# First layer of an attention and two-layer MoE kernel: the high and low part of g taken one step later, pieces of x every three steps

## The chip, the cores and the metric

The kernel runs on one core of a Trainium2 chip. The metric is the device time of one execution in microseconds; the time of the kernel before is the median of three runs. TensorE, VectorE, ScalarE and GpSimd are called PE, DVE, ACT and POOL in the rows of the profile, SyncE (which issues most DMAs) SP.

## The reference

Three pieces follow each other. Attention with a feature map: q and k (8 batches, 8 heads, 576 positions, 64 wide) go through exp(+p - max) and exp(-p + max) of p = x @ w_phi, and the output is num / den. The result is x, 4608 tokens by 512. The **first layer**, in which the change lies, is

```
h = x @ w_in           # 4608 x 2048
g = h - tanh(h)
y = g @ w_out          # 4608 x 512
```

The second layer computes ((y @ w1) * (y @ w2)) @ w3 @ w_out2. All of it is fp32.

## The kernel before, in words

A product in fp32 is made of three matmuls with operands of a rounded type (float32r): each operand is split into a high part (a copy into the rounded type) and a low part (the rest), and high x high, low x high, high x low are added up in PSUM.

The first layer (`moe1`) works through 9 blocks of 512 tokens, and in each through 16 chunks of 128 columns of h; one chunk of one block is a step, n = 0 to 143. In step n, TensorE gets `mm1(n)` (L456: 12 matmuls, x and w_in give the tile h(n), 128x512, in one of three PSUM banks) and then `mm2(n - 2)` (L522: 12 matmuls that add g(n-2) @ w_out to four y banks; the four gl matmuls come last, except in the first and last chunk of a block). At the end of a block the four y banks are copied out, three by ScalarE and one by VectorE (`y_out`, L508; three buffers `yo`), and stored to DRAM. The last two steps hold two tiles of the next product, `w34` (L682), in the place of mm1.

Between them lies `act_g` (L479), which makes g: ScalarE takes u = h*h (L485), t = tanh(h) (L486), s (L487) and the mask m (L488); VectorE takes t = h - t (L491), then u by two operations (L492, L494; a polynomial for small h) and puts u into t where the mask says so (L495). Then ScalarE copies t into its high part gh (L503), and GpSimd subtracts gh from t to get the low part gl (L504). u and t have two buffers, s and m one, gh two, gl three.

The order of each engine's work is the order in which the program is written; nothing reorders it. Beside g, each step carries "extras" from a table by step (`extra`): the conversion and splitting of the weights of both layers, in pieces of 128x256. Of these, ScalarE's operations (L105, L120, L127, and L566 for the high part of a split) are issued in `act_g` before gh; VectorE's (L109, L112, L115), GpSimd's (L123 adds, L570 low parts, L589 to L598 sums) and SyncE's (loads of raw weights, stores of w at L601 and L620) are issued after `act_g`. In steps 14 to 77 groups of seven steps combine weights for the second layer (`combos`): on GpSimd four adds, four sums and seven splits for each group. Later steps split single pieces.

Last in a step comes the next block's x, in four pieces. Piece k is loaded in chunk 4k (`load_x`, one DMA for the numerators and two or four for the reciprocals of the denominators, from SyncE's queue into single buffers xn and xr), multiplied on GpSimd in chunk 4k + 1 (L875) and split in chunk 4k + 2 (`split_x`: high part on ScalarE, L881; low part on GpSimd, L882). The last split is thus issued in chunk 14. The first tile of the next block needs all four pieces.

Of the kernel before, what the change touches and what calls it, by code (L numbers as in the profile page):

```python
# [9 lines left out]
F32R = mybir.dt.float32r  # L10
# [42 lines left out]
def kernel(ctx, tc, qk_in, v_in, w_phi, w_in, w_out, w12, w3t_in, wo2, out):  # L53
# [24 lines left out]
    def space(kind, i, shape, dt=F32R):  # L78
        if kind == "x":
            pool = xpools[i // NK]  # L80
        else:
            pool = wpool if i < FC_EARLY else late[0]
        return pool.tile(shape, dt, tag=f"{kind}{i}", name=f"{kind}{i}")
# [51 lines left out]
    def fc_view(t):  # L135
        return t.rearrange("p k f -> p (k f)")
# [319 lines left out]
    def mm1(n):  # L456
        j, i = divmod(n, NFC)
        hh[n] = mm_x(xs[j], slots["in", i], "h")
# [11 lines left out]
    def moe1():  # L470
        with ExitStack() as es:
            p1 = es.enter_context(tc.tile_pool(name="m1", bufs=1))
            p2 = es.enter_context(tc.tile_pool(name="m2", bufs=2))
            p3 = es.enter_context(tc.tile_pool(name="m3", bufs=2))
            ps_y = es.enter_context(tc.tile_pool(name="ps_y", bufs=1, space=PSUM))

            gg, yy = {}, {}

            def act_g(n, ys):  # L479
                h = hh[n]  # L480
                u = p2.tile([128, 512], F32, tag="u", name="u")
                s = p1.tile([128, 512], F32, tag="s", name="s")
                t = p2.tile([128, 512], F32, tag="t", name="t")
                m = p1.tile([128, 512], F32, tag="m", name="m")
                ACT.activation(u, h, ACTF.Square)  # L485
                ACT.activation(t, h, ACTF.Tanh)  # L486
                ACT.activation(s, u, ACTF.Square, bias=c1_sb)  # L487
                ACT.activation(m, u, ACTF.Relu, bias=lim_sb, scale=-1.0)  # L488
                for d in range(3):
                    y_out(ys, d)  # L490
                DVE.tensor_tensor(t, h, t, ALU.subtract)  # L491
                DVE.scalar_tensor_tensor(u, h, C2, u, ALU.mult, ALU.mult)  # L492
                y_out(ys, 3)
                DVE.scalar_tensor_tensor(u, s, C0, u, ALU.add, ALU.mult)  # L494
                DVE.copy_predicated(t, m.bitcast(U32), u)  # L495

                x = extra.get(n, [])
                for f in x:
                    if f in on_act:
                        f()  # L500
                gh = p3.tile([128, 512], F32R, tag="gh", name="gh")
                gl = p3.tile([128, 512], F32R, tag="gl", name="gl", bufs=3)
                ACT.activation(gh, t, ACTF.Copy)  # L503
                POOL.tensor_tensor(gl, t, gh.bitcast(F32), ALU.subtract)  # L504
                del hh[n]
                gg[n] = gh, gl

            def y_out(ys, d):  # L508
                if ys is None:
                    return  # L510
                j, pss = ys
                if d == 3 and j == NB - 1:
                    t = p2.tile([128, 512], F32, tag="t", name="t")
                else:
                    t = p1.tile([128, 512], F32, tag="yo", name="yo", bufs=3)
                if d < 3:
                    ACT.activation(t, pss[d], ACTF.Copy)
                else:
                    DVE.tensor_copy(t, pss[d])
                (ACT if d < 3 else SP).dma_start(y_d[d * 128:(d + 1) * 128, j * 512:(j + 1) * 512], t)  # L520

            def mm2(n):  # L522
                j, i = divmod(n, NFC)
                if i == 0:
                    yy[j] = [ps_y.tile([128, 512], F32, tag=f"y{d}", name=f"y{d}") for d in range(NK)]
                wh, wl = slots["out", i]
                gh, gl = gg.pop(n)
                todo = [(d, m) for d in range(NK) for m in range(3)]
                if 0 < i < NFC - 1:

                    todo.sort(key=lambda a: a[1] == 2)
                for d, m in todo:
                    w, x = ((wh, gh), (wl, gh), (wh, gl))[m]
                    PE.matmul(  # L534
                        yy[j][d], w[:, d * 128:(d + 1) * 128], x,
                        start=i == 0 and m == 0, stop=i == NFC - 1 and m == 2,
                    )
                return (j, yy.pop(j)) if i == NFC - 1 else None
# [3 lines left out]
            cw = 256  # L542
# [17 lines left out]
            def split(of, store):  # L560
                o2 = {}

                def s_hi():
                    t = of()
                    w = o2["w"] = p2.tile([128, 2, cw], F32R, tag="w", name="w")
                    ACT.activation(w[:, 0], t, ACTF.Copy)  # L566

                def s_lo():
                    w = o2["w"]
                    POOL.tensor_tensor(w[:, 1], of(), w[:, 0].bitcast(F32), ALU.subtract)  # L570

                def s_store():
                    store(o2["w"].bitcast(F32))

                on_act.add(s_hi)
                return [[s_hi, s_lo, s_store]]
# [71 lines left out]
            n_all = NB * NFC  # L648
            LAG = 2
            for n in range(n_all + LAG):  # L650
                j, i = divmod(n, NFC)
                if n < n_all:
                    mm1(n)
                else:
                    w34(n - n_all)
                ys = mm2(n - LAG) if n >= LAG else None
                if n >= n_all:
                    for d in range(4):
                        y_out(ys, d)
                if n < n_all:  # L660
                    act_g(n, ys)
                    for f in extra.get(n, []):
                        if f not in on_act:
                            f()
                    if j + 1 < NB:
                        if i % 4 == 0:
                            xa = load_x(j + 1, i // 4)
                        if i % 4 == 1:
                            mul_x(*xa)
                        if i % 4 == 2:  # L670
                            split_x(j + 1, i // 4, xa[0])
                    if j + 1 == NB and i == 2:
                        load_b(0)
                i = n - (n_all - NFC + 1)
                if 0 <= i < NFC:
                    w3t[i] = space("wi", i, [128, 8, 128])
                    SP.dma_start(fc_view(w3t[i]).bitcast(F32), w3t_d[i % 2][i // 2])
                i -= LAG
                if 0 <= i < 8:
                    slots["wo2", i] = slot("wo", i, [128, DM])  # L680
                    for e in range(2):
                        SP.dma_start(slots["wo2", i][e].bitcast(F32), wo2_d[e][i])  # L682

    def w34(i):
        ps = ps_h.tile([128, 512], F32, tag="h", name="h")
        th, tl = w3t.pop(2 * i), w3t.pop(2 * i + 1)
        m = 0
        for j in range(8):
            xh, xl = slots["wo2", j]
            for a, x in ((th, xh), (tl, xh), (th, xl)):  # L690
                PE.matmul(ps, a[:, j, :], x, start=m == 0, stop=m == 23)
                m += 1
        hl = slots["w34", i] = slot("wo", 8 + i, [128, DM])
        ACT.activation(hl[0], ps, ACTF.Copy)
        DVE.tensor_tensor(hl[1], ps, hl[0].bitcast(F32), ALU.subtract)
# [149 lines left out]
    with tc.manual_schedule():  # L845
# [5 lines left out]
        hh, ab_ps, w3t, pending = {}, {}, {}, []  # L851
# [5 lines left out]
        def load_x(j, kk):  # L857
            a = xn.tile([128, 512], F32, tag="xn", name="xn")
            r = xn.tile([128, 512], F32, tag="xr", name="xr")
            c0 = j * 512  # L860
            SP.dma_start(a, num_d[kk * 128:(kk + 1) * 128, c0:c0 + 512])
            done = 0
            while done < 512:
                bp, o = divmod(c0 + done, PT)
                n = min(512 - done, PT - o)
                for e in range(2):
                    SP.dma_start(
                        r[e * D:(e + 1) * D, done:done + n],
                        rden_d[bp, 2 * kk + e:2 * kk + e + 1, o:o + n].to_broadcast([D, n]),
                    )  # L870
                done += n
            return a, r

        def mul_x(a, r):
            POOL.tensor_tensor(a, a, r, ALU.mult)  # L875

        def split_x(j, kk, a):
            hi, lo = slot("x", NK * (j % 2) + kk, [128, 512])
            for e, p in enumerate(xs.setdefault(j, [[None] * NK, [None] * NK])):
                p[kk] = (hi, lo)[e]  # L880
            ACT.activation(hi, a, ACTF.Copy)  # L881
            POOL.tensor_tensor(lo, a, hi.bitcast(F32), ALU.subtract)  # L882
# [56 lines left out]
```

## Time and profile before

| what | value |
|---|---|
| median of 3 runs | 1845.81 us (1845.61 to 1847.29) |
| the profiled execution's own time | 1846.37 us |
| its span | 1844.3 us |
| TensorE busy | 1761.6 us, 96% of the span |
| VectorE, ScalarE, GpSimd busy | 1078.6, 881.5, 902.2 us |

The span runs from the first to the last instruction of the profiled execution; its own time has some 2 us around that. Busy times are sums over stages with different limits. For a change in one stage the waits of that stage have to be read. The granted clock of TensorE is a share of its upper level, 2.4 GHz.

### The profile page before, as it was taken

The page shows a single profiled execution, that of the slowest core. Times are in us where ns is not written, and L with a number is a line of the kernel's source. Part 1 is how long each engine was busy: PE and PEld are TensorE (multiplying, and loading weights), DVE is VectorE, ACT ScalarE, POOL GpSimd, SP SyncE. Part 2 cuts the span into 40 slices and gives each one's busy share as a digit, 9 for nine tenths or more (in the row PEclk, how much of TensorE's full clock was granted, in tenths as well). Part 3 has the DMA queues.
Part 4 walks back from the last instruction along what each step waited for, and adds up shares of the span by engine and source line. Part 5 has one row for each costly group of instructions (what it writes and reads, how often), then busy time and mean ns, then how long its engine had stood idle before and what let it go on. Part 6 is the DMA issues. An engine that isn't in the chain of part 4 may idle for free.

```text
span 1844.3 us, 29297 instructions
## 1 busy us (share of the span) xinstructions
PE 1761.6 (96%) x10464; PEld 1447.3 (78%) x10464; DVE 1078.6 (58%) x1728; ACT 881.5 (48%) x1775; POOL 902.2 (49%) x902
## 2 busy tenths in 40 slices
PE   7999899999998989899999999999999999999999
PEld 5666666668777777677878777888999999999998
DVE  6777787747666656656666766552444444444442
ACT  4656566647656565656666766552121212121211
POOL 5767677726465655655554545231333333333321
PEclk9999999999999999999999999999999999999999
DMA  4444445422223232233334342634647474747461
GB/s 154 144 146 152 148 154 175 125 56 70 70 97 109 97 107 94 96 105 100 121 107 122 103 120 92 228 112 144 204 151 238 151 238 150 236 151 239 151 204 64
DMA packets 143200, 254.68 MB, mean 138 GB/s; under 512 B 18384, under 2 KB 48464, under 8 KB 143056
## 3 DMA queue, kind: packets, MB, share of 16 engines
q1 hardware_dynamic: 139008, 245.68, 41.8%
q10 hardware_dynamic: 4048, 7.15, 1.1%
q8 instruction: 83, 1.36, 0.3%
q14 instruction: 61, 0.50, 0.1%
HBM read 196.89 MB, written 55.87 MB: 137 GB/s over the span
## 4 chain that ended last, share of the span: by engine, by line
PE 50%; issue 14%; POOL 11%; DVE 10%; ACT 8%; DMA 6%; SPq 2%; POOLq 0%; DVEq 0%; ACTq 0%
PE o L796 11%; PE pb L748 8%; PE pa L748 5%; PE pc L748 5%; PE y L534 4%; PE p L200 3%; PE h L465 3%; PE o L331 3%; POOL gl L504 3%; POOL w L570 2%; DVE u L494 2%; DVE t L495 2%; POOL et L123 2%; PE kv L278 2%; PE o L340 2%
## 5 line engine op out<-in xcount | busy, mean ns | idle before, releaser
L465 PE MATMUL h<-x,wi 128*128 128x512 f32 x1728 | 420.9, 391 | 28.1 <-POOL x L882 20.2
L465 PEld LDWEIGHTS h<-x,wi 128*128 128x128 f32 x1728 | 324.4, 188 | 102.1 <-POOL x L882 23.7
L504 POOL TENSOR_TENSOR gl<-t,gh 128x512 fp32r<-128x512 f32 x144 | 186.4, 1294 | 411.2 <-ACT gh L503 385.1
L534 PE MATMUL y<-gh,wo 128*128 128x512 f32 x1152 | 308.3, 403 | 15.6 <-ACT gh L503 13.0
L534 PEld LDWEIGHTS y<-gh,wo 128*128 128x128 f32 x1152 | 219.7, 193 | 75.2 <-ACT gh L503 26.1
L787 POOL TENSOR_TENSOR c<-c,c 128x384 f32<-128x384 f32 x48 | 67.6, 1408 | 322.6 <-DVE c L785 322.6
L491 DVE TENSOR_TENSOR t<-h,t 128x512 f32<-128x512 f32 x144 | 99.6, 692 | 203.8 <-ACT t L486 203.8
L503 ACT ACTIVATE gh<-t 128x512 fp32r<-128x512 f32 x144 | 90.9, 631 | 231.0 <-DVE t L495 228.1
L748 PE MATMUL pb<-wi,w 128*128 128x384 f32 x864 | 173.8, 335 | 3.3 <-DVE u L775 3.3
L534 PE MATMUL y<-gl,wo 128*128 128x512 f32 x576 | 165.4, 394 | 0.7 <-POOL gl L504 0.7
L748 PEld LDWEIGHTS pb<-wi,w 128*128 128x128 f32 x864 | 151.8, 188 | 5.6 <-DVE u L775 5.6
L207 DVE TENSOR_REDUCE m<-p 128x4 f32<-128x512 f32 (+1 forms) x145 | 98.7, 681 | 78.1 <-PE p L200 77.9
L492 DVE SCALAR_TENSOR_TENSOR u<-h,u 128x512 f32<-128x512 f32 x144 | 99.6, 692 | 70.6 <-ACT m L488 70.6
L220 ACT ACTIVATE kp<-dk 128x512 f32<-128x512 f32 x144 | 83.0, 626 | 109.1 <-DVE dk L209 77.7
L494 DVE SCALAR_TENSOR_TENSOR u<-s,u 128x512 f32<-128x512 f32 x144 | 128.2, 890 | 4.6
L534 PEld LDWEIGHTS y<-gl,wo 128*128 128x128 f32 x576 | 110.5, 192 | 24.9 <-POOL gl L504 1.1
L495 DVE COPY_PREDICATED t<-m,u 128x512 f32<-128x512 uint32 x144 | 125.8, 874 | 4.9
L748 PE MATMUL pa<-wi,w 128*128 128x384 f32 x576 | 116.4, 336 | 0.0
L748 PE MATMUL pc<-wi,w 128*128 128x384 f32 x576 | 115.3, 334 | 0.0
L775 DVE TENSOR_TENSOR u<-pb,c 128x384 f32<-128x384 f32 x48 | 26.8, 558 | 147.9 <-PE pb L748 138.1
L302 POOL TENSOR_TENSOR ks<-ks,kp 128x256 f32<-128x256 f32 x128 | 96.4, 779 | 21.3 <-ACT kp L220 21.3
L262 ACT ACTIVATE qp<-tr 128x512 f32<-128x512 f32 (+2 forms) x224 | 84.2, 446 | 45.3 <-PE tr L241 24.7
(104 smaller groups left out, 3130.0 us busy)
## 6 DMA issues: line engine op xcount, KB each, us to landing
w<-w_d SPq DMA_DIRECT2D x336, 256.0 KB
qk<-in_qk SPq DMA_DIRECT2D x33, 576.0 KB
w_d<-w SPq DMA_DIRECT2D x56, 256.0 KB
v<-in_v SPq DMA_DIRECT2D x32, 320.0 KB
num_d<-st SPq DMA_DIRECT2D x128, 72.0 KB
xn<-num_d SPq DMA_DIRECT2D x36, 256.0 KB
x<-y_d SPq DMA_DIRECT2D x24, 384.0 KB
out<-o SPq DMA_DIRECT2D x36, 256.0 KB
```

Source lines behind the costliest of these rows:

```text
L207: DVE.tensor_reduce(m[:, :n], what[g][:, j], AX.X, ALU.max, apply_absolute_value=True)
L302: POOL.tensor_tensor(s, kp[m // G][:, :, m % G, :] if t < 4 else s, x, ALU.add)
L465: PE.matmul(ps, a[:, kk, :], b[kk], start=m == 0, stop=m == 3 * NK - 1)
L491: DVE.tensor_tensor(t, h, t, ALU.subtract)
L492: DVE.scalar_tensor_tensor(u, h, C2, u, ALU.mult, ALU.mult)
L494: DVE.scalar_tensor_tensor(u, s, C0, u, ALU.add, ALU.mult)
L495: DVE.copy_predicated(t, m.bitcast(U32), u)
L503: ACT.activation(gh, t, ACTF.Copy)
L504: POOL.tensor_tensor(gl, t, gh.bitcast(F32), ALU.subtract)
L534: PE.matmul(yy[j][d], w[:, d * 128:(d + 1) * 128], x, start=i == 0 and m == 0, stop=i == NFC - 1 and m == 2,)
L748: PE.matmul(ps, w[:, a, c], x[b][:, kk, :], start=start and m == 0, stop=m == 5, skip_group_check=True)
L796: PE.matmul(ps, a[:, cols], w, start=i == 0 and m == 0, stop=i == 7 and m == 2)
```

## The change

In `act_g` the copy gh and the subtraction gl are cut out and put into a function of their own, `g_parts(n)`. `act_g(n)` calls `g_parts(n - 1)` right after its own four ScalarE operations, ahead of the y copies and of the extras. After the last step `g_parts` is called once more, behind the first tile of the next product and ahead of `mm2`. gl has two buffers now, w three. The pieces of x are loaded, multiplied and split in chunks 3k, 3k + 1 and 3k + 2, so that the last split is issued in chunk 11.

```diff
@@ -474,7 +474,7 @@
             p3 = es.enter_context(tc.tile_pool(name="m3", bufs=2))
             ps_y = es.enter_context(tc.tile_pool(name="ps_y", bufs=1, space=PSUM))
 
-            gg, yy = {}, {}
+            gg, yy, tt = {}, {}, {}
 
             def act_g(n, ys):
                 h = hh[n]
@@ -486,6 +486,7 @@
                 ACT.activation(t, h, ACTF.Tanh)
                 ACT.activation(s, u, ACTF.Square, bias=c1_sb)
                 ACT.activation(m, u, ACTF.Relu, bias=lim_sb, scale=-1.0)
+                g_parts(n - 1)
                 for d in range(3):
                     y_out(ys, d)
                 DVE.tensor_tensor(t, h, t, ALU.subtract)
@@ -498,11 +499,17 @@
                 for f in x:
                     if f in on_act:
                         f()
+                del hh[n]
+                tt[n] = t
+
+            def g_parts(n):
+                if n < 0:
+                    return
+                t = tt.pop(n)
                 gh = p3.tile([128, 512], F32R, tag="gh", name="gh")
-                gl = p3.tile([128, 512], F32R, tag="gl", name="gl", bufs=3)
+                gl = p3.tile([128, 512], F32R, tag="gl", name="gl")
                 ACT.activation(gh, t, ACTF.Copy)
                 POOL.tensor_tensor(gl, t, gh.bitcast(F32), ALU.subtract)
-                del hh[n]
                 gg[n] = gh, gl
 
             def y_out(ys, d):
@@ -562,7 +569,7 @@
 
                 def s_hi():
                     t = of()
-                    w = o2["w"] = p2.tile([128, 2, cw], F32R, tag="w", name="w")
+                    w = o2["w"] = p2.tile([128, 2, cw], F32R, tag="w", name="w", bufs=3)
                     ACT.activation(w[:, 0], t, ACTF.Copy)
 
                 def s_lo():
@@ -653,6 +660,8 @@
                     mm1(n)
                 else:
                     w34(n - n_all)
+                if n == n_all:
+                    g_parts(n - 1)
                 ys = mm2(n - LAG) if n >= LAG else None
                 if n >= n_all:
                     for d in range(4):
@@ -663,12 +672,12 @@
                         if f not in on_act:
                             f()
                     if j + 1 < NB:
-                        if i % 4 == 0:
-                            xa = load_x(j + 1, i // 4)
-                        if i % 4 == 1:
+                        if i % 3 == 0 and i < 12:
+                            xa = load_x(j + 1, i // 3)
+                        if i % 3 == 1 and i < 12:
                             mul_x(*xa)
-                        if i % 4 == 2:
-                            split_x(j + 1, i // 4, xa[0])
+                        if i % 3 == 2 and i < 12:
+                            split_x(j + 1, i // 3, xa[0])
                     if j + 1 == NB and i == 2:
                         load_b(0)
                 i = n - (n_all - NFC + 1)
```

## Rows read from the trace of the kernel before

**Rows 1.** Windows: length, busy time of PE, PEld, DVE, ACT, POOL, clock, DMA share, GB/s
```profile
387.37:1254.17 866.80, 822.43 (x3509) 662.87 (x3505) 541.17 (x865) 540.27 (x1080) 453.41 (x452) 0.98 0.33 106
472.40:1147.22 674.82, 636.02 (x2689) 509.94 (x2688) 434.18 (x696) 430.60 (x872) 377.21 (x384) 0.97 0.32 103
```

**Rows 2.** Timeline of PE at the layer's start: start us, us, what
```profile
401.54 2.88 PE L465 MATMUL h<-x,wi 128*128 128x512 f32 x12
404.26 1.98 PE L534 MATMUL y<-gh,wo 128*128 128x512 f32 x8
406.98 2.88 PE L465 MATMUL h<-x,wi 128*128 128x512 f32 x12
```

**Rows 3.** Waits of PE in the layer: us in total, times, longest us
```profile
PE h L465 <- POOL x L882: 20.2, 8, 4.5
PE y L534 <- ACT gh L503: 13.0, 16, 1.9
PE h L465 <- ACT x L881: 7.9, 8, 1.6
PE y L534 <- DVE yo L519: 2.4, 3, 1.4
```

**Rows 4.** Timeline of PE: the first and the eighth block border
```profile
472.40 2.20 PE L465 MATMUL h<-x,wi 128*128 128x512 f32 x9
478.67 3.19 PE L534 MATMUL y<-gh,wo 128*128 128x512 f32 x8
483.02 2.92 PE L465 MATMUL h<-x,wi 128*128 128x512 f32 x12
...
1147.22 2.20 PE L465 MATMUL h<-x,wi 128*128 128x512 f32 x9
1156.22 2.88 PE L465 MATMUL h<-x,wi 128*128 128x512 f32 x12
```

**Rows 5.** Waits of ACT in the layer
```profile
ACT gh L503 <- DVE t L495: 228.1, 130, 3.9
ACT w L566 <- DMA w_d<-w: 58.9, 38, 2.9
```

**Rows 6.** Timeline of ACT: one step
```profile
749.05 0.63 ACT L503 ACTIVATE gh<-t 128x512 fp32r<-128x512 f32 x1 [1.70 <-DVE t L495]
...
750.06 0.59 ACT L486 ACTIVATE t<-h 128x512 f32<-128x512 f32 x1
...
751.15 0.72 ACT L488 ACTIVATE m<-u,cs 128x512 f32<-128x512 f32 x1
...
754.22 0.63 ACT L503 ACTIVATE gh<-t 128x512 fp32r<-128x512 f32 x1 [1.69 <-DVE t L495]
```

**Rows 7.** Lines of DVE: ns min/median/max, first and last start us
```profile
L492 DVE SCALAR_TENSOR_TENSOR u<-h,u x137: 691/692/694, 432.8 to 1237.9; 128x512 f32<-128x512 f32 x137
...
L494 DVE SCALAR_TENSOR_TENSOR u<-s,u x138: 680/693/1817, 426.9 to 1238.6; 128x512 f32<-128x512 f32 x138
...
L495 DVE COPY_PREDICATED t<-m,u x138: 731/756/1841, 428.5 to 1239.3; 128x512 f32<-128x512 uint32 x138
...
L115 DVE SCALAR_TENSOR_TENSOR et<-eraw,et x88: 401/413/1528, 429.2 to 1142.9; 128x256 uint32<-128x256 uint32 x88
```

**Rows 8.** Timeline: DVE and POOL at once
```profile
715.35 1.82 DVE L494 SCALAR_TENSOR_TENSOR u<-s,u 128x512 f32<-128x512 f32 x1
...
715.32 1.29 POOL L875 TENSOR_TENSOR xn<-xn,xr 128x512 f32<-128x512 f32 x1
```

**Rows 9.** Groups of POOL in the layer: busy us, mean ns, idle before
```profile
L504 POOL TENSOR_TENSOR gl<-t,gh 128x512 fp32r<-128x512 f32 x144 | 186.4, 1294 | 411.2 <-ACT gh L503 385.1 <-DMA xr<-rden_d 24.6 <-DMA w3th_d<-w 1.4
L570 POOL TENSOR_TENSOR w<-et,w 128x256 fp32r<-128x256 f32 x104 | 76.0, 741 | 0.0
...
L882 POOL TENSOR_TENSOR x<-xn,x 128x512 fp32r<-128x512 f32 x32 | 43.1, 1346 | 0.0
```

**Rows 10.** Waits of DVE in the layer
```profile
DVE yo L519 <- DMA y_d<-yo: 25.6, 8, 5.0
```

## The prediction

> **What bounds the kernel now.** I began with the page: TensorE is busy for 96% of the span, so I asked where the missing part lies. The busy time by stretch shows it: the first layer, from its first matmul at 387.37 us to its last at 1254.17, takes 866.80 us, of which TensorE is busy for 822.43, at a mean granted clock of 0.98 of the upper level, 2.4 GHz [rows 1]: 44 of the some 83 idle microseconds of the span lie here. With nothing in the way a step (24 matmuls, two tiles' halves) takes 5.44 us, as from 401.54 to 406.98 [rows 2]. The layer has 144 steps, and two blocks of 24 matmuls of the next product lie inside the stretch: 146 x 5.44 = 794.2 us. So 72.6 us are lost here, and this is all that the change can win.
>
> The waits of TensorE and its timeline say where. (a) At each of the eight block borders the first tile of the new block waits for its last piece of x, first for ScalarE's high part, then for GpSimd's low part: 7.9 and 20.2 us of pure idling in 8 borders [rows 3]. A border step lasts from 472.40 to 483.02, 10.62 us, in the first and 9.00 us in the eighth [rows 4]; the eight add up to 89.1, that is 45.5 us above 8 x 5.44. More than the idling, because after the wait the clock falls to 1.2 GHz: eight y matmuls that took 1.98 us at 404.26 took 3.19 us at 478.67 [rows 2, 4]. (b) At the start tile 0 comes late: 36 + 12 matmuls need 10.88 us from 387.37, so 398.25, and the next step starts at 401.54 [rows 2]: 3.3 us. (c) y matmuls wait for VectorE's copy of the fourth y bank, 2.4 us [rows 3]. (d) The rest, 72.6 - 45.5 - 3.3 - 2.4 = 21.4 us, is inside the blocks: y matmuls waiting for gh, with the slow clock behind them [rows 3].
>
> (a) and (d) have one root. ScalarE, in step n, does four operations, then gh of the same tile, which waits for VectorE's last operation on t: 228.1 us in 130 waits [rows 5]. So ScalarE, VectorE, ScalarE form a closed loop, a step of which takes 749.05 to 754.22, 5.17 us, with nothing else in it [rows 6]. That is 0.27 us below TensorE's 5.44. Everything that gets into the loop (the copy w waiting for its store, 58.9 us in 38 waits [rows 5]; L494 held up by GpSimd, up to 1817 ns instead of 693 [rows 7]) makes the chain late, and it catches up only 0.27 us a step. The pieces of x ride in the same late queues.
>
> **The change, part by part.**
>
> *gh and gl a step later.* The same 144 ACTIVATEs and 144 GpSimd subtractions; none is added, none has a DMA. gh(n-1) now follows m(n) on ScalarE, when VectorE has long finished t(n-1): the 228.1 us of waits go, and the loop opens. What is left as a cycle is m(n+1) behind L495(n), which still reads the one m buffer, then L492, L494, L495: at the medians 0.72 + 0.69 + 0.69 + 0.76 us, about 2.9, far below 5.44 [rows 6, 7]. ScalarE's own work, 430.6 us in seven blocks, is 3.8 us a step [rows 1]. So ScalarE keeps up, and (d) goes: -21.4 us. y(n) needs gh(n) 10.88 us after tile n's matmuls; it is ready at about 5.44 + 2.9. This cover is 2.5 us; before it was about 5.
>
> *What then is late next: gl.* It now stands on GpSimd behind the previous step's extras and in front of VectorE's L494. Two things follow. First, every gl now meets L494 of the next tile. The timeline shows what this costs: L494 began 0.03 us after a 1.29 us GpSimd operation and lasted 1.82 us [rows 8], 1.13 us more. L492, one of whose inputs is in PSUM, never took over 694 ns [rows 7], and L491 is of that kind too. VectorE has 3.88 us of work a step (434.18 over 112 steps [rows 1]) and takes 1.13 more within 5.44. Second, the queue ahead of gl. In a step with the most extras GpSimd begins behind VectorE's part of a conversion: ScalarE's four operations (0.5 + 1.81), L492 0.69, L494 1.82, L495 0.76, L115 0.41, so 6.0 us after the tile's matmuls [rows 6 to 8]. Then an add, two splits and a sum at 0.74 each, a piece of x 1.35, gl 1.29 [rows 9]: 11.6 us, and with L494 and L495 of the next tile let in between (1.45) 13.1. y's low matmuls want gl at 10.88 + 1.8 = 12.7. So most steps have room, and the heaviest two of each group of seven are late by 0.4 us, the second of them by more, as it begins late. There are 8 groups. Lower bound zero (it fits), upper bound in rival B; I take 1.5 us for each group, 12 us: nearer to zero, as only two steps in seven are near the limit.
> Against the change speaks a rule of the Trainium skill, SBUF — State Buffer, section SBUF: two separate sides: VectorE, with two SBUF inputs, and GpSimd hold one port pair by an exclusive lock for the whole instruction, and whoever comes second is blocked fully. By it the sum of both would be the bound, as in rival B, and the result some 1820; the trace agrees in the main, but after the other's end, at 716.61, L494 needed 0.56 us, not its 0.69, so a part of it ran beside [rows 8].
>
> *Pieces of x every three steps.* The last split is issued in step 11, not 14: three steps earlier, 16.3 us, against losses of 5.2 us at the first border and 3.6 at the eighth [rows 4]. (a) goes: -45.5 us. The same number of GpSimd and ScalarE operations per block; the first twelve steps bear 12/16 more densely (2 x 1.35 us per 3 steps, not 4: +0.2 us a step), which is in the sum above. Of SyncE's DMAs a piece has one load of x and two to four of the reciprocals; they wait till the piece before has been split, now one step earlier instead of two, and behind them wait raw weights and the stores of w. Weights are used two steps after their load, 10.9 us, so I count nothing; with that cover gone ScalarE would wait as it does for w now, up to 2.9 us a time [rows 5].
>
> *Three w buffers, two gl.* The third w takes the store out of ScalarE's order; its 58.9 us were part of (d), so no term of its own. gl's third buffer isn't missed: gl(n) is written from about 8.3 us after tile n's matmuls on, and gl(n-2) has been read at 2.72.
>
> *What the later order costs.* At the start gh(0) comes behind m(1): +0.6 us (0 to 0.7, one m [rows 6]). At each border the y copies on ScalarE come behind a gh, up to 0.63 us later [rows 6], and the fourth copy on VectorE waits for the first copy's store (25.6 us in 8 waits [rows 10]), which already stalled TensorE three times. Between 0 and 8 x 0.63 = 5 us; I take 3, as five borders had room. At the end gh(143) stands behind one copy of the next product, under 5.44 us of matmuls: nothing.
>
> **Sum,** against the profiled execution's own 1846.4 us (span 1844.3; the median of the runs is 1845.8, 0.6 below, which I leave): 1846.4 - 45.5 - 21.4 + 0.6 + 3 + 12 = 1795.1. Of it 1780 is left with all added terms at zero.
>
> **The rivals.**
>
> *B: VectorE and GpSimd become the bound.* In blocks 1 to 7 GpSimd is busy for 377.21 and VectorE for 434.18 us of 112 steps [rows 1]: 3.37 + 3.88, and without L491 and L492, which run beside GpSimd, 5.87 us a step if the rest excludes each other. This is above 5.44; but it counts blocked time on both sides (L494 and L495 are longer than their medians because of it). At the full 5.87, 112 x 0.43 = 48 us replace the 12: 1831. For it: the extra 1.13 us a step. Against: the double count, and that fixed parts overlap. I put it at 1808 to 1832, in the middle 1820.
>
> *C: slower, by a new loop over two steps.* t has two buffers, and Tanh of tile n+2 may write only when gl(n) has read t. The loop: Tanh to m's end 1.81 [rows 6], L492 0.69, L494 1.82, L495 1.84, L115 0.41 (its median) [rows 7], add, two splits and sum 2.96, x 1.35, gl 1.29 [rows 9]: 12.2 us for two steps, 6.1 a step. In all 112 steps that is 0.66 x 112 = 74 us, and 1846.4 - 66.9 + 3.6 + 74 = 1857. It decides from 12.0 us per two steps on. Against it: the terms are the longest of a step, and of L494 and L495 the longest of their rows; at the medians and one add and split it is under 8.
>
> *D: the pieces of x stay late,* if their loads, one buffer deep, lag behind SyncE's queue: (a) remains, 1846.4 - 21.4 + 15.6 = 1841. Against: three steps are 16 us.
>
> **How the numbers follow.** A, the sum, 0.58, with 1782 to 1808 as its own range; B 0.27; C 0.08; D 0.05; 0.02 for no change by something unnamed. A measurement here can tell 0.2%, 3.7 us. Faster: A, B and part of D, 0.88; same 0.04; slower 0.08. The predicted time is A's, 1795. The range of 8 in 10 is A with most of B: 1781 to 1826.
>
> **What would show it.** In the profile after: no wait of h matmuls for x; gh no longer waiting for VectorE; border steps near 5.5 to 7 us; L494's mean risen from 890 ns toward 1.5 us or more; the waits left on TensorE being y for gl and y for VectorE's yo copy. Wrong it would be if steps inside the blocks average over 5.7 us with VectorE or GpSimd without gaps (B), if Tanh waits for gl (C), or if h still waits for x (D).

## The result, and the profile after

The changed kernel takes 1788.95 us (median; 1785.67 to 1790.13), before 1845.71 beside it: a ratio of 0.9689 (95% interval 0.9672 to 0.9705), 56.8 us faster. The forecast was 1795.1, from 1781 to 1826. The profiled execution took 1788.79 us (span 1787.0).

Window of the first layer after, from its first matmul to its last (columns as in [rows 1]):

```profile
386.11:1197.27 811.16, 800.33 (x3508) 657.52 (x3505) 690.05 (x865) 544.83 (x1080) 501.26 (x452) 1.00 0.35 113
```

It answers to the first of [rows 1]: 866.80 us have become 811.16, 55.6 us less, which is nearly the whole difference of the two profiled executions (1846.37 - 1788.79 = 57.6). Above the 794.2 us of undisturbed matmuls 17.0 are left of 72.6; the mean granted clock went from 0.98 to 1.00. VectorE's busy time rose by 149 us and GpSimd's by 48, with the same number of instructions.

Waits in the layer after (us in total, times, longest). The change shifts the line numbers: L511 is now gh, L512 gl, L541 the y matmuls, L526 the fourth y copy, L573 the copy w.

```profile
ACT u L485 <- PE h L465: 175.1, 110, 2.6
...
ACT t L486 <- POOL gl L512: 17.9, 26, 1.8
...
DVE yo L526 <- DMA y_d<-yo: 11.4, 3, 5.3
...
ACT w L573 <- DMA w_d<-w: 10.4, 15, 1.7
...
PE y L541 <- POOL gl L512: 6.6, 9, 1.9
...
PE y L541 <- ACT gh L511: 2.5, 1, 2.5
...
PE y L541 <- DVE yo L526: 1.7, 1, 1.7
```

The reader should see the direction of the first line. Before, ScalarE stood before gh and waited for VectorE, 228.1 us [rows 5]; now it waits for TensorE's h, in 110 of 144 steps: TensorE leads, ScalarE follows. No matmul of h waits for x any more, where 16 did [rows 3]. What TensorE still waits for is, in the main, gl, 6.6 us in 9 waits; one of them, 0.68 us, is at the start, as before the change.

Groups of VectorE in the layer, two of before and then those after (busy us, mean ns, idle before):

```profile
L494 DVE SCALAR_TENSOR_TENSOR u<-s,u 128x512 f32<-128x512 f32 x144 | 128.2, 890 | 4.6
L495 DVE COPY_PREDICATED t<-m,u 128x512 f32<-128x512 uint32 x144 | 125.8, 874 | 4.9
```
```profile
L495 DVE SCALAR_TENSOR_TENSOR u<-s,u 128x512 f32<-128x512 f32 x144 | 203.5, 1413 | 4.7
L496 DVE COPY_PREDICATED t<-m,u 128x512 f32<-128x512 uint32 x144 | 167.2, 1161 | 5.0
L493 DVE SCALAR_TENSOR_TENSOR u<-h,u 128x512 f32<-128x512 f32 x144 | 98.4, 684 | 31.5 <-ACT m L488 31.2
```

L495 is the L494 of before, L496 the L495: their means rose from 890 and 874 ns to 1413 and 1161. L493 reads h from PSUM and does not rise: 684 ns, 692 before. The timeline of one step shows VectorE's L495 beside GpSimd's gl:

```profile
491.62 1.73 DVE L495 SCALAR_TENSOR_TENSOR u<-s,u 128x512 f32<-128x512 f32 x1
```
```profile
491.50 1.30 POOL L512 TENSOR_TENSOR gl<-t,gh 128x512 fp32r<-128x512 f32 x1
```

gl starts 0.12 us ahead and ends at 492.80; L495 needs 0.55 us more from there. It is the picture of [rows 8], and it is now the common case: the median of L495 is 1660 ns, where that of L494 was 693 [rows 7].

Two of the steps that are still late on TensorE, and GpSimd's queue ahead of the first:

```profile
500.30 2.88 PE L465 MATMUL h<-x,wi 128*128 128x512 f32 x12
503.02 1.97 PE L541 MATMUL y<-gh,wo 128*128 128x512 f32 x8
505.36 1.20 PE L541 MATMUL y<-gl,wo 128*128 128x512 f32 x4 [0.37 <-POOL gl L512]
506.40 2.89 PE L465 MATMUL h<-x,wi 128*128 128x512 f32 x12
509.12 1.97 PE L541 MATMUL y<-gh,wo 128*128 128x512 f32 x8
512.03 1.20 PE L541 MATMUL y<-gl,wo 128*128 128x512 f32 x4 [0.93 <-POOL gl L512]
```
```profile
500.16 0.75 POOL L123 TENSOR_TENSOR et<-et,eraw 128x256 uint32<-128x256 uint32 x1 [1.05 <-ACT t L486]
500.86 1.49 POOL L577 TENSOR_TENSOR w<-et,w 128x256 fp32r<-128x256 f32 x2
502.32 1.26 POOL L599 TENSOR_TENSOR et<-et 128x256 f32<-128x256 f32 x1
503.54 1.76 POOL L512 TENSOR_TENSOR gl<-t,gh 128x512 fp32r<-128x512 f32 x1
```

An add, two splits, a sum and only then gl, which ends at 505.30; y's low matmuls start at 505.36. That is the heavy step of the prediction.

### The profile page after: what moved, and what is told of

It is laid out like the page before. It is cut to its first block, busy times and chain, and to the rows that moved or that the text cites. A ratio compares the mean times of both kernels' runs of the same rounds, so it can differ in the third digit from the quotient of the medians.

```text
span 1787.0 us, 29379 instructions
## 1 busy us (share of the span) xinstructions
PE 1738.9 (97%) x10464; PEld 1441.8 (81%) x10464; DVE 1225.2 (69%) x1728; ACT 886.3 (50%) x1775; POOL 950.9 (53%) x902
## 4 chain that ended last, share of the span: by engine, by line
PE 80%; DVE 8%; issue 4%; DMA 4%; POOL 2%; ACT 1%; SPq 1%; DVEq 0%; POOLq 0%; ACTq 0%
PE h L465 18%; PE y L541 18%; PE o L805 11%; PE pb L757 8%; PE pa L757 5%; PE pc L757 5%; PE p L200 4%; PE o L331 3%; PE kv L278 2%; PE o L340 2%; DMA xr<-rden_d 1%; PE tr L241 1%; PE h L700 1%; DVE u L495 1%; PE kv L317 1%
## 5 line engine op out<-in xcount | busy, mean ns | idle before, releaser
L465 PE MATMUL h<-x,wi 128*128 128x512 f32 x1728 | 415.1, 389 | 0.0
L541 PE MATMUL y<-gh,wo 128*128 128x512 f32 x1152 | 294.7, 390 | 4.2 <-ACT gh L511 2.5
L512 POOL TENSOR_TENSOR gl<-t,gh 128x512 fp32r<-128x512 f32 x144 | 202.0, 1403 | 177.6 <-ACT gh L511 118.7
L541 PEld LDWEIGHTS y<-gh,wo 128*128 128x128 f32 x1152 | 216.5, 188 | 50.7 <-ACT gh L511 3.4
L495 DVE SCALAR_TENSOR_TENSOR u<-s,u 128x512 f32<-128x512 f32 x144 | 203.5, 1413 | 4.7
L485 ACT ACTIVATE u<-h 128x512 f32<-128x512 f32 x144 | 85.8, 596 | 181.8 <-PE h L465 175.1
L541 PE MATMUL y<-gl,wo 128*128 128x512 f32 x576 | 165.0, 393 | 6.6 <-POOL gl L512 6.6
L496 DVE COPY_PREDICATED t<-m,u 128x512 f32<-128x512 uint32 x144 | 167.2, 1161 | 5.0
L541 PEld LDWEIGHTS y<-gl,wo 128*128 128x128 f32 x576 | 107.6, 188 | 33.3 <-POOL gl L512 11.4
L123 POOL TENSOR_TENSOR et<-et,eraw 128x256 uint32<-128x256 uint32 x92 | 68.9, 749 | 113.5 <-ACT u L485 33.3
L493 DVE SCALAR_TENSOR_TENSOR u<-h,u 128x512 f32<-128x512 f32 x144 | 98.4, 684 | 31.5 <-ACT m L488 31.2
```

The costliest lines, as they stand in the source:

```text
L465: PE.matmul(ps, a[:, kk, :], b[kk], start=m == 0, stop=m == 3 * NK - 1)
L541: PE.matmul(yy[j][d], w[:, d * 128:(d + 1) * 128], x, start=i == 0 and m == 0, stop=i == NFC - 1 and m == 2,)
```

## The experiments

All medians are beside their own runs of the kernel before (1845.4 to 1846.7 us).

**Which part of the change did it?** The pieces of x alone, on the kernel before:

```diff
-                        if i % 4 == 0:
-                            xa = load_x(j + 1, i // 4)
+                        if i % 3 == 0 and i < 12:
+                            xa = load_x(j + 1, i // 3)
...
```

> Only the pieces of x every three steps, g as before. Theory 1 (the terms of the prediction add up): the waits at the block borders go, the rest stays: 1800 us (1795 to 1808), no h matmul waits for x. Theory 2 (one root: the closed loop through ScalarE and VectorE takes longer than TensorE's 5.44 us a step, and the border wait is only the place where its lateness comes out): the loop sets the time as before, 1840 us (1833 to 1846), and the waits of TensorE move from h for x to y for gh.

1840.32 us, ratio 0.9973 (0.9962 to 0.9985): theory 2 holds. TensorE's waits in the layer:

```profile
PE y L534 <- ACT gh L503: 18.8, 27, 1.9
...
PE y L534 <- ACT yo L517: 11.2, 8, 2.6
...
PE y L534 <- DVE yo L519: 6.6, 5, 2.0
```

No h waits for x, exactly as the change promised, and some 5 us are won. Of the 28.1 us of border waits 21 came back as waits for gh and for the y copies (36.6 us in these three lines, 15.4 before [rows 3]), which stand in the same late queues of ScalarE and VectorE. TensorE's timeline shows the move: the first steps of the eight later blocks, 45.5 us above 8 x 5.44 before, are 0.8 us above it, and the third steps, whose y matmuls need the banks copied out, rose from 3.5 to 30.2 us above it. One of them:

```profile
685.30 0.73 PE L534 MATMUL y<-gh,wo 128*128 128x512 f32 x2 [2.62 <-ACT yo L517]
```

In the changed kernel the same copies stand one gh later on ScalarE, and the third steps are only 2.2 us above: the copies came late here because the queue was late. gh still waits for VectorE:

```profile
ACT gh L503 <- DVE t L495: 223.7, 128, 3.7
```

The other half, gh and gl a step later with the new buffers, and x every four steps as before:

```diff
-                        if i % 3 == 0 and i < 12:
-                            xa = load_x(j + 1, i // 3)
+                        if i % 4 == 0:
+                            xa = load_x(j + 1, i // 4)
...
```

> gh and gl a step later with the buffers of the change, pieces of x every four steps as before. Theory 1 (terms add): the border waits stay, 1828 us (1822 to 1836). Theory 2 (one root): with the loop open the pieces come in time even from step 14 on, 1790 us (1786 to 1797); h waits for x for under 8 us in all.

1789.52 us, 0.9693 (0.9675 to 0.9711): all of it. One wait for x is left in the whole layer:

```profile
PE y L541 <- POOL gl L512: 3.8, 6, 1.9
...
PE h L465 <- POOL x L891: 1.2, 1, 1.2
```

So the two parts don't add up: alone they give 5.0 and 55.8 us, together about 56. The border wait was where the lateness of the closed loop came out, not a cost of its own. With the step later, gh also came to stand ahead of the extras on ScalarE; no run separates the two.

**How much of the loop was the store of w?** The kernel before with three buffers w and two gl:

```diff
-                gl = p3.tile([128, 512], F32R, tag="gl", name="gl", bufs=3)
+                gl = p3.tile([128, 512], F32R, tag="gl", name="gl")
...
-                    w = o2["w"] = p2.tile([128, 2, cw], F32R, tag="w", name="w")
+                    w = o2["w"] = p2.tile([128, 2, cw], F32R, tag="w", name="w", bufs=3)
```

> The kernel before with three buffers w (and two gl, for the room), nothing else. It tells how much of the 58.9 us of waits of the copy w for its store was on the closed loop. Theory 1 (on the loop wherever it outlasts VectorE's work on t, as at 765 us, where gh began some 0.7 us late for it; about 20 steps): 1832 us (1826 to 1838), and gh's waits for t grow by most of what w's waits lose. Theory 2 (wholly beside VectorE's work): 1844 to 1846. Theory 3 (all of it on the loop): under 1800.

1841.79 us, 0.9976 (0.9965 to 0.9988): 4.9 us, between theories 1 and 2, and outside both.

```profile
ACT gh L503 <- DVE t L495: 231.5, 126, 3.7
...
ACT w L566 <- DMA w_d<-w: 19.9, 12, 2.5
...
ACT w L566 <- POOL et L595: 15.0, 7, 2.5
...
ACT w L566 <- POOL et L598: 9.1, 8, 1.3
```

w's waits for the store fell from 58.9 to 19.9 us, but 24 of the 39 us that went came back as waits for the sums on GpSimd that make w's source. Most of the waits that went had this second cause behind them. I had looked at one such step, 765 us, and taken it for twenty.

In the changed kernel the third w is worth hardly anything:

```diff
-                    w = o2["w"] = p2.tile([128, 2, cw], F32R, tag="w", name="w", bufs=3)
+                    w = o2["w"] = p2.tile([128, 2, cw], F32R, tag="w", name="w")
```

> The change with two buffers w instead of three. Theory 1 (ScalarE has over 1 us to spare in a step): the waits of the copy w for its store grow to 30 to 60 us, and the time stays within 2 us of the change, 1787 to 1791. Theory 2: the waits come in the fullest steps, where there is nothing to spare: 1794 us or more, with more waits of y for gl.

1790.46 us, 0.9699 (0.968 to 0.9718), theory 1; the waits of w grew to 28.3 us in 34, a little less than expected.

**Is the new loop through t's two buffers (rival C) a cost?** Three t, for which one w has to go:

```diff
-                t = p2.tile([128, 512], F32, tag="t", name="t")
+                t = p2.tile([128, 512], F32, tag="t", name="t", bufs=3)
...
-                    w = o2["w"] = p2.tile([128, 2, cw], F32R, tag="w", name="w", bufs=3)
+                    w = o2["w"] = p2.tile([128, 2, cw], F32R, tag="w", name="w")
```

> Two buffers w and three t, to be read beside the run with two w alone. Theory 1 (rival C of the prediction is there, but hidden): Tanh's waits for gl, 17.9 us in the change, go to nearly nothing, and the time stays within 2 us of two w alone. Theory 2 (rival C costs something): 4 us or more below two w alone, with the waits of y for gl under half.

1793.23 us, 0.9712 (0.9695 to 0.973). Tanh's waits for gl, 13.3 us with two w alone, are gone from the list, and the median lies 2.8 us above that of two w alone, not below. The intervals of the two overlap, so I read no loss from it; the gain of theory 2 is not there, and theory 1 holds but for the size. y still waits 6.8 us for gl.

**How much room have GpSimd and VectorE left?** Every gl computed twice:

```diff
                 POOL.tensor_tensor(gl, t, gh.bitcast(F32), ALU.subtract)
+                POOL.tensor_tensor(gl, t, gh.bitcast(F32), ALU.subtract)
```

> The change with every gl computed twice in a row on GpSimd, same result: 1.29 us of GpSimd's time more in each step, ahead of y. Theory 1 (VectorE and GpSimd exclude each other in the main, and of a step's 5.44 us about 15% are free): the two become the bound in the steps with extras, 1830 us (1815 to 1850). Theory 2 (full exclusion for whole instructions, 5.87 us a step already): over 1900. Theory 3 (GpSimd has 310 us of idle time in the layer and nothing else counts): 1789 to 1797.

1883.68 us, 1.02 (1.0187 to 1.0213): slower than the kernel before, and 34 us beyond the upper end of theory 1. 144 subtractions more, at 1.29 us each [rows 9], cost 94.7 us over the change, 0.66 us a step; so, as an estimate, on the average only 0.63 us of a step of 5.44 was free, 12%.

```profile
ACT t L486 <- POOL gl L513: 155.2, 112, 3.2
...
PE y L542 <- POOL gl L513: 68.6, 61, 3.2
```

Here rival C shows in full: Tanh waits for gl in 112 steps. Whether that costs the time or only shows where it goes, the third t tells:

```diff
-                t = p2.tile([128, 512], F32, tag="t", name="t")
+                t = p2.tile([128, 512], F32, tag="t", name="t", bufs=3)
...
                 POOL.tensor_tensor(gl, t, gh.bitcast(F32), ALU.subtract)
+                POOL.tensor_tensor(gl, t, gh.bitcast(F32), ALU.subtract)
...
-                    w = o2["w"] = p2.tile([128, 2, cw], F32R, tag="w", name="w", bufs=3)
+                    w = o2["w"] = p2.tile([128, 2, cw], F32R, tag="w", name="w")
```

> Every gl twice, as in the run before, but with three buffers t and two w. Theory 1 (what cost 95 us there is rival C, Tanh waiting for gl to have read t: 155 us of such waits): with the third t these waits go and most of the loss with them, 1800 to 1830 us. Theory 2 (VectorE and GpSimd, excluding each other, are the bound, and Tanh's wait is only where it shows): within 10 us of 1884.

1876.25 us, 1.0169 (1.0154 to 1.0184): 7.4 us less, theory 2. The waits of Tanh are gone, y's waits for gl are not:

```profile
PE y L542 <- POOL gl L513: 64.7, 61, 3.2
```

So Tanh's wait is mostly where the loss shows and not its cause; what TensorE waits for is gl, the last in GpSimd's queue. In the stretch with most extras GpSimd is busy for 424 of 495 us, VectorE for 410:

```profile
505.00:1000.00 495.00, 450.35 (x1896) 356.05 (x1895) 409.75 (x478) 307.40 (x612) 424.44 (x360) 0.99 0.30 99
```

How much of these busy times is one engine blocked by the other was not separated: no run took the blocking away and left the work. So it stays open which of the two engines is the bound, or whether it is only both together.

**Would gl be better on VectorE?** Behind L496 of the next tile:

```diff
                 DVE.copy_predicated(t, m.bitcast(U32), u)
+                if low:
+                    low.pop()()
...
-                POOL.tensor_tensor(gl, t, gh.bitcast(F32), ALU.subtract)
                 gg[n] = gh, gl
+                low.append(lambda: DVE.tensor_tensor(gl, t, gh.bitcast(F32), ALU.subtract))
...
```

> The change with gl on VectorE, behind L496 of the next tile, instead of GpSimd. GpSimd loses 186 us and the mutual blocking falls: L495 from 1413 ns to under 1000, L496 from 1161 to under 950. Theory 1 (the queue on GpSimd ahead of gl is what is left to lose): y no longer waits for gl, 1783 us (1780 to 1786). Theory 2 (VectorE, with 100 us more of its own, is now late with gl): 1789 or more, with y waiting for gl from VectorE.

1825.28 us, 0.9886 (0.9871 to 0.9901): theory 2, and far more than 1789. The blocking did fall (L495 from 1413 to 763 ns; L496 from 1161 to 1012, not under 950 as expected). The loss sits mostly at the block borders: the third steps of the eight later blocks are 37.3 us above 8 x 5.44, 2.2 in the change. Here are TensorE and VectorE in one of them:

```profile
683.80 0.79 PE L546 MATMUL y<-gl,wo 128*128 128x512 f32 x1 [5.26 <-DVE gl L516]
```
```profile
679.47 0.69 DVE L531 COPY yo<-y 128x512 f32<-128x512 f32 x1 [3.75 <-DMA y_d<-yo]
...
682.01 1.74 DVE L516 TENSOR_TENSOR gl<-t,gh 128x512 fp32r<-128x512 f32 x1
```

gl is caught behind the fourth y copy, which waits for a store. So it was tried only where GpSimd is fullest and no border is near:

```diff
+            full = [14 + 7 * g + i for g in range(8) for i in (5, 6)]
+            full = [n for n in full if n % NFC > 1]
...
+                if n in full:
+                    low.append(lambda: DVE.tensor_tensor(gl, t, gh.bitcast(F32), ALU.subtract))
+                else:
...
```

> The change, but in the two fullest steps of each group of seven (not beside a block border) gl goes to VectorE, behind L496 of the next tile; 14 of 144. Theory 1 (what is left inside the blocks is GpSimd's queue ahead of gl): y's waits for gl, 6.6 us, fall to under 2, and the time to 1783 us (1781 to 1786). Theory 2 (VectorE is as full there): 1788 or more.

1788.72 us, 0.9695 (0.968 to 0.9709); the changed kernel, run again beside it:

> The changed kernel as it is, for comparison on the same chip: 1789 us (1786 to 1791) by every theory.

1789.36 us, 0.9696 (0.9681 to 0.971). No difference, theory 2 of the run before: of the 6.6 us of waits 5.0 are left, one half of them now for VectorE's gl.

```profile
PE y L548 <- POOL gl L520: 2.6, 2, 1.9
...
PE y L548 <- DVE gl L518: 2.4, 4, 1.0
```

**The order at the start and at the borders.** g of tile 0 split at once, and the y copies ahead of gh where there are any:

```diff
-                g_parts(n - 1)
+                if ys is None:
+                    g_parts(n - 1)
                 for d in range(3):
                     y_out(ys, d)
+                if ys is not None:
+                    g_parts(n - 1)
...
                 tt[n] = t
+                if n == 0:
+                    g_parts(0)
...
```

> The change with two places moved: g of tile 0 is split at once, in its old place, and at a block's end the three y copies stand ahead of gh on ScalarE. Theory 1 (the start's 5.4 us go back to 3.3, and the border waits for the fourth y copy shrink by up to 0.6 us each): 1786 us (1783 to 1788). Theory 2 (the start is set by the shared work of VectorE and GpSimd, and the y copies by their stores): within 1 us of the change, 1788 to 1790.

1800.53 us, 0.9749 (0.9737 to 0.9762): 11.6 us worse, which neither theory allows. TensorE at one border:

```profile
665.38 2.88 PE L465 MATMUL h<-x,wi 128*128 128x512 f32 x12
669.95 0.73 PE L546 MATMUL y<-gh,wo 128*128 128x512 f32 x2 [1.69 <-ACT gh L516]
671.56 0.50 PE L546 MATMUL y<-gl,wo 128*128 128x512 f32 x1 [0.88 <-POOL gl L517]
```

The next y matmuls need gh of that tile at once, and gl two matmuls later, for a block's first chunk takes them bank by bank. The three y copies with a DMA each, and a wait for a store of w, hold ScalarE from 665.05 to 669.26 here, and gh begins only then. The third steps of the eight later blocks are 15.7 us above 8 x 5.44, 2.2 in the change, which covers the whole loss. So the change has this order right. At the start nothing was won either: from the first matmul to the fourth tile 16.21 us, 16.25 in the change, and the step behind it took 0.8 us more.

## Why the prediction was right, and where it was not

**The sum** was 1795.1, the result 1788.95, 6 us lower and inside case A's own range. 21.3 us should be left over in the layer (72.6 - 66.9 + 0.6 + 3 + 12), 17.0 were. TensorE's timeline splits them: 5.4 us at the start (forecast 3.9), 8.2 in the eight steps in which y waits for gl (12), 2.2 in the third steps of the blocks (5.4, for the fourth y copy), some 1.2 elsewhere. The added terms missed both ways, so that the sum fits within 6 us is in part luck.

**The step that failed is the split of the 66.9 us.** The prediction put 45.5 us on the step "pieces of x every three steps" and 21.4 on the loop's opening. The runs give 5.0 us for the former alone, and 55.8 for the latter alone. The text had found the root, the closed loop through ScalarE and VectorE, then priced the two places where it came out as if each had its own cure. It also took the loop to be 0.27 us faster than TensorE, from one step with L494 and L495 near their medians. With their means, 890 and 874 ns, the same loop comes to some 5.49 us (an estimate: 5.17 + 0.20 + 0.12), above 5.44 before any wait of w: what the border no longer cost, the loop cost elsewhere. The sum held because the change contains the cure of the root; for x alone the same working would have forecast 1800, and 1840 came.

**gl behind the extras:** 12 us were forecast for the heavy pairs. Inside the blocks y waits 5.9 us for gl, in eight steps that are 8.2 us above 5.44 in sum. Seven of the eight belong to the heavy pairs; the eighth comes later, at 884 us. Place, order and mechanism are as told, the size was too large.

**L494 under gl:** told as near 1.5 us or more, 1413 ns came; VectorE took the rest within its step, as worked out. The Trainium skill, SBUF — State Buffer, section SBUF: two separate sides, has the loser of the shared port blocked for the whole instruction. The rows agree with the blocking (0.55 us of L495 remain after gl's end), but the sum of both engines that I drew from it, some 1820 us, did not come.

**The start** cost 2.1 us more, not 0.6: 386.11 + 10.88 is 396.99, and the fourth tile began at 402.36. y's wait for gh(0) is 0.63 us longer than before, as forecast; the rest is the clock, which fell to 1.2 GHz after the longer wait (2.53 us, 1.90 before), as it had not before. From the first gl matmul to the fourth tile, with no wait in between, 3.85 us pass, before 2.41.

```profile
397.10 0.73 PE L541 MATMUL y<-gh,wo 128*128 128x512 f32 x2 [2.53 <-ACT gh L511]
...
400.39 1.05 PE L541 MATMUL y<-gh,wo 128*128 128x512 f32 x2
...
402.36 2.90 PE L465 MATMUL h<-x,wi 128*128 128x512 f32 x12
```

Two y matmuls that took 0.63 us before take 1.05 there. The windows give the granted clock, 0.51 of the upper level in this stretch and 1.00 after it (before, it was 1.00 from 396 to 401.5 us):

```profile
398.40:401.70 3.30, 3.19 (x8) 2.52 (x9) 3.23 (x5) 2.22 (x4) 1.75 (x2) 0.51 0.02 5
402.40:410.00 7.60, 7.60 (x35) 6.29 (x34) 6.60 (x9) 4.58 (x10) 4.88 (x5) 1.00 0.31 87
```

**The borders** were to cost 3 us more; the waits of y for the fourth copy went from 2.4 to 1.7 us. The copies came later, as told, but the rest of VectorE's and ScalarE's queue was no longer late.

**Rivals.** B did not come true, but it was near: by the estimate above, 0.63 us of GpSimd's time a step separated the change from it. C's waits are there (17.9 us) and cost nothing measurable. The prediction lets C's loop decide from 12.0 us for two steps on; two steps of TensorE are 10.88, so by its own working it would bind from there. D, late x, is excluded: even pieces every four steps come in time, but for one wait of 1.2 us, once gh comes a step later.

## What to carry to other kernels

Waits of one engine at several places can have one root: ask first whether the engines that feed it run in a closed loop, each waiting for the other within a tile, and how long that loop is beside the consumer's step. If it is as long, prices of single waits don't add, and moving the victim's work earlier wins little; delaying the last link by one tile opens the loop. Before loading an engine that slows another, as GpSimd does VectorE here, measure the room left by doubling an operation: here 1.29 us more on GpSimd undid the whole gain.

## What the runs showed of the hardware that was not expected

GpSimd is idle for 38% of the layer in the changed kernel (501.26 of 811.16 us busy), yet by the estimate above only 0.63 us a step could have been added without cost. VectorE's TENSOR_SCALAR L112 (128x256) rose from a mean of 304 to 734 ns although it has one input tile, while L109, of the same kind, went from 312 to 333. In the step of 500 us L112 begins 0.10 us behind the start of GpSimd's add L123 and ends 0.14 us behind its end; that this is the same blocking as L495's was not tested:

```profile
L112 DVE TENSOR_SCALAR et<-et 128x256 uint32<-128x256 uint32 x92 | 67.5, 734 | 3.2
```
